# Block-sparse attention and a gated FFN in one kernel: keys dealt six to a partition, the first tile's mask added by TensorE, and a new table of scheduling priorities

## The chip, the cores and the metric

The kernel runs on one core of one Trainium2 chip. The metric is the device time of one execution in microseconds (us); the kernel before takes 277.04 us, the median of ten runs (276.79 to 277.46). Next to the times stands one profiled execution, from which all durations below are taken.

## The reference

Attention with a block mask, and behind it a feed-forward layer with a Swish gate:

```
B, H, S, D = 4, 8, 768, 64          # q, k, v: float32
scores = q @ k^T / sqrt(D)
mask   = blocks of 32: |i-j| <= 1, first and last block row and column,
         and three sampled key blocks for each query block
attn   = softmax(where(mask, scores, -1e9)) @ v        # [B, H, S, D]
x      = attn.transpose(0, 2, 1, 3).reshape(3072, 512)
h      = x @ w_in                                      # w_in  [512, 2048]
g      = h * sigmoid(beta * h)
out    = g @ w_out                                     # w_out [2048, 512]
```

The mask is the same for all batches and heads; only `sampled_blocks` (24x3 integers) makes it depend on an input.

## The kernel before

**Attention.** Two heads of a batch make a pair; there are sixteen pairs x, four to a batch. q, k and v of a pair are loaded as float32 into staging tiles `st_q`, `st_k`, `st_v`, cast to float16 on DVE or POOL (`s_q`, `s_k`, `va`), and q and k are turned so that the head's 64 features lie on partitions (`qX`, `kX`). The first four pairs are turned on PE and copied out of PSUM ("turn", "turn cp"); the others by a transposing DMA from SP's queue. A token (or key) index is written as (group g of 3, partition p of 128, c of 2): two neighbouring rows stand on a partition, so one piece of a load is 2 x 64 x 4 = 512 bytes.

A unit is one pair and one query tile, of n = 256 or 512 queries; batch 0 has a 256 tile and then a 512 tile, and each has four units. A unit's score step ("sc") makes one double bank of PSUM, 128 keys by 1024 scores for two heads; the two heads' matmuls use 64 rows of the array each. With n = 256 a unit has three steps of four 256-column matmuls, with n = 512 six steps of two 512-column matmuls. ACT takes the exponential of a step ("ex", tile `et`, 128x1024), DVE multiplies it with the 0/1 mask `mask01` ("mk"). When all steps of a unit are masked, PE multiplies with v ("av", 24 matmuls of 65 columns for each 256 queries; the 65th column holds the sums), DVE takes reciprocals and scales ("norm", tile `xst`), and the result is turned (on PE for batch 0 and the last pair, else by a transposing DMA) into `xT_sb`.

**The mask.** `sampled_blocks` is loaded first; a few small DVE operations make a 24x24 block mask, PE turns it, PE spreads it over key partitions with the `onehot` matrix (built on POOL at the start), and three copies on POOL ("spread") widen it to `mask01`, 128 x 3 x 384.

**The FFN.** `add_moe` handles a block of 256 or 512 tokens: sixteen groups of four matmuls with `w_in` ("hp"), a tanh on ACT for each ("th"), a multiply on DVE ("gm", tile `g`), then for each 128 tokens sixteen matmuls with `w_out` ("op"), a copy to `osb` on ACT or DVE, and a store from SP. The blocks are 256, five times 512, and 256 tokens. The weights are loaded and cast by four DMAs from POOL's queue of 2 MB of HBM data each. The first is held back by a one-element POOL copy that waits for the key load of pair 3 (`W_GATE`), and the loads of pair 4 are held back the same way until halves of `w_out` are there.

**The order.** All this is entered as nodes with engine, duration, dependencies and buffers, and `order_of` writes out one order for all engines by a list scheduling: of the nodes that can start it takes the one with the least start time plus a bias for its kind (`BIAS`). `MOST` limits how many PSUM banks a kind may hold, `SLOTS` gives the number of buffers of each tile. Each engine then runs its list in order; semaphores do the waiting. Nearly all operations are recorded through one helper and show as line 208 in the profile; the loads are lines 474 and 477, the weight loads 452 and 458, POOL's casts 497, the transposing DMAs 514 and 666, the stores 725.

Of the kernel before, what the change touches and what calls it, by code (L numbers as in the profile page):

```python
# [23 lines left out]
class Node:  # L24


    def __init__(self, kind, eng, dur, lat, emit, deps=(), take=(), use=(), moved=0,
                 rows=128, port=False, at=0.0, place=0.0):
        self.kind, self.place = kind, place
        self.eng = eng if isinstance(eng, tuple) else (eng,)  # L30
        self.dur = dur if isinstance(dur, dict) else {e: dur for e in self.eng}
        self.tail, self.emit = lat, emit
        self.deps = [d if isinstance(d, tuple) else (d, 0.0) for d in deps if d is not None]
        self.take, self.use, self.moved = list(take), list(take) + list(use), moved
        self.rows, self.port, self.at = rows, port, at
        for b in self.use:
            b.users += 1
        self.start = self.done = self.on = None


BIAS = {"av": -69, "beta": -455, "cast": 94, "dma": -1239, "ex": 257, "gm": -727, "hp": -468,
        "load": 1496, "lone sc": 331, "mask": -1415, "mk": 241, "next sc": 94, "norm": -152,
        "op": -13, "op on": -70, "osb": 284, "sc": -204, "spread": -316, "th": 422,
        "turn": -3422, "turn cp": -88, "two sc": -72, "weights": 774, "x cp": -31,
        "x turn": -102}

W_GATE = (3, "k")
# [12 lines left out]
MOST = {"av": 8, "hp": 6, "sc": 3}  # L60
# [31 lines left out]
def order_of(nodes, free, slots):  # L92
# [7 lines left out]
    left, after, at_dep = {}, {}, {}  # L100
    todo = []
# [8 lines left out]
    while todo:  # L110
        best = None
        for n in todo:
# [21 lines left out]
            for e in n.eng:  # L134
# [3 lines left out]
                bias = BIAS[n.kind]  # L138
                if n.rows == 64:
                    if rows == 64:  # L140
                        bias += BIAS["next sc"]
                    else:
                        room = sum(whole(bank, d, n_start) for d in range(len(bank) // 2))
                        bias += BIAS["lone sc"] if room < 2 else BIAS["two sc"] if room < 3 else 0
# [12 lines left out]
        if n.moved:  # L157
            other = "POOL" if e == "SP" else "SP"
            t, rest, rate = max(wire[e], start + DMA_FIRST[e]), n.moved, RATE[e]
            if e == "SP" and wire[other] > t:  # L160
                both = min(rest, (wire[other] - t) * SHARED)
                wire[other] += both / RATE[other]
                t, rest = t + both / SHARED, rest - both
            wire[e] = t + rest / rate
            n.done = wire[e] + DMA_LAST
        else:
# [74 lines left out]
def kernel(  # L241
# [29 lines left out]
    SLOTS = {"st_k": 2, "st_q": 5, "st_v": 5, "s16_k": 4, "s16_q": 2, "set": 4, "va": 4,  # L271
             "et": 13, "xst": 5, "recip": 7, "t_sb": 6, "g": 2, "osb": 3, "sc": 4}
# [36 lines left out]
    onehot = persist.tile([NB, NG, P], FP16, name="onehot")  # L309
    mask16 = persist.tile([NB, NB], FP16, name="mask16")  # L310
    mask_t = persist.tile([NB, NB], FP16, name="mask_t")
    mask_kb = persist.tile([P, NG, NB], FP16, name="mask_kb")
    mask01 = persist.tile([P, NG, NG * P], FP16, name="mask01")
# [23 lines left out]
    def emit_first():  # L337
# [6 lines left out]
        nc.vector.memset(warm, 0.0)  # L344

# [7 lines left out]
        nc.gpsimd.memset(onehot, 1.0)  # L353
        nc.gpsimd.affine_select(out=onehot, in_=onehot, pattern=[[CG * P, NG], [CG, P]],
                                compare_op=ALU.is_ge, fill=0.0, base=0,
                                channel_multiplier=-BLK)
        nc.gpsimd.affine_select(out=onehot, in_=onehot, pattern=[[-CG * P, NG], [-CG, P]],
                                compare_op=ALU.is_ge, fill=0.0, base=BLK - 1,
                                channel_multiplier=BLK)
# [15 lines left out]
    nodes = []  # L375

    def add(*a, **kw):
        n = Node(*a, **{"place": len(nodes) * 1e-3, **kw})
        nodes.append(n)
        return n  # L380

    mask_of = {}

    def add_mask():
# [3 lines left out]
        def mb(eng):  # L388
            dve.tensor_copy(out=sb_f32, in_=sb_i32)
            for r in range(3):  # L390
                dve.scalar_tensor_tensor(out=mask_blk if r < 2 else mask16, in0=iota_j,
                                               scalar=sb_f32[:, r:r + 1], in1=mask_blk,
                                               op0=ALU.is_equal, op1=ALU.max)

        def mt():
            pe.matmul(at(tb)[0:NB, 0:NB], lhsT=mask16, rhs=identity[0:NB, 0:NB],
                             start=True, stop=True)
# [4 lines left out]
        def km():  # L402
            for g in range(NG):
                pe.matmul(at(kb)[:, g * NB:(g + 1) * NB], lhsT=onehot[:, g], rhs=mask_t,
                                 start=True, stop=True)

        def kmc(eng):
            copy_on(eng)(out=mask_kb.rearrange("p c j -> p (c j)"), in_=at(kb)[:, 0:NG * NB])
# [8 lines left out]
        def spread(eng, g):  # L417
# [6 lines left out]
                    [P, NG, P // w, w]))  # L424
        n_mb = add("mask", "DVE", 950, 90, mb, at=4200.0)
        n_mt = add("mask", "PE", 60, 200, mt, deps=[n_mb], take=[tb], rows=32)
        n_mtc = add("mask", ("ACT", "DVE"), {"ACT": 200, "DVE": 100}, 100, mtc, deps=[n_mt], use=[tb])
        n_km = add("mask", "PE", 350, 200, km, deps=[n_mtc], take=[kb], rows=32)
        n_kmc = add("mask", ("ACT", "DVE"), {"ACT": 250, "DVE": 220}, 100, kmc, deps=[n_km], use=[kb])
        for g in range(NG):  # L430
            mask_of[g] = add("mask" if g == 0 else "spread", ("DVE", "POOL"),
                             {"DVE": 460, "POOL": 450}, 80,
# [11 lines left out]
    def add_weights(gate):  # L444
        st, load = gate

        def shut():
            nc.gpsimd.tensor_copy(out=w_in_sb[0:1, 0, 0:1], in_=at(st)[0:1, 0, 0:1])
        gate = add("weights", "POOL", 600, 50, shut, deps=[load], use=[st])
        for i in range(2):  # L450
            def wi(i=i):
                nc.gpsimd.dma_start(out=w_in_sb[:, :, i * 1024:(i + 1) * 1024],
                                    in_=w_in_r[:, :, i * 1024:(i + 1) * 1024])
            w_in_of[i] = add("weights", "POOL", 1000, 0, wi,
                            deps=[gate if i == 0 else (w_in_of[0], -1e9)], moved=2097152, port=True)
        for i in range(2):
            def wo(i=i):
                nc.gpsimd.dma_start(out=w_out_sb[:, i * 8:(i + 1) * 8, :],
                                    in_=w_out_r[:, i * 8:(i + 1) * 8, :])
            w_out_of[i] = add("weights", "POOL", 1200, 0, wo, deps=[(w_in_of[1], -1e9)],  # L460
                              moved=2097152, port=True)
# [4 lines left out]
    def add_load(nm, x, st, lo, hi, gate, more=False):  # L466
# [3 lines left out]
        def load():  # L470
            hg = src[b, 2 * j:2 * j + 2].rearrange("h (g p c) d -> p (h g) (c d)", g=NG, p=P)
# [6 lines left out]
        deps = [(d, -1e9) for d in last_load + begin]  # L478
        kw = {"use" if more else "take": [st]}
        if gate is not None:  # L480
            def shut():
                nc.gpsimd.tensor_copy(out=at(st)[0:1, 0, lo * D:lo * D + 1],
                                      in_=w_out_sb[0:1, gate * 8, 0:1])
            deps.append(add("weights", "POOL", 600, 50, shut, deps=[w_out_of[gate]], take=[st]))
            kw = {"use": [st]}
        last_load[:] = [add("load", "SP", 500 if hi - lo in (NC, CG) else 1000, 0, load, deps=deps,
                             moved=68000 * (hi - lo) + (170000 if x == 0 and nm == "v" else 0),
                             **kw)]
        return last_load[0]
# [13 lines left out]
    def add_half(x, nm, kq, lo, hi, first, gate, at_work=None):  # L503
# [4 lines left out]
        load = add_load(nm, x, st, lo, hi, gate, at_work and lo > 0)  # L508
        if x < NPAIR and lo == 0:
            loads[x, nm] = st, load  # L510
# [22 lines left out]
    def add_prep(x, gates=(None, None, None)):  # L533
# [18 lines left out]
        if x < NPAIR:  # L552
            loads[x, "v"] = st, lv
# [7 lines left out]
    def tile_steps(x, q0, n):  # L561
# [5 lines left out]
        for kc0 in range(0, NC, kn):  # L567
# [3 lines left out]
            def mm(sc=sc, kc0=kc0):  # L571
                kX, qX = at(kq)
                for i in range(kn):
                    for hh in range(2):
                        pe.matmul(
                            at(sc)[:, hh, i * n:(i + 1) * n],
# [3 lines left out]
                            start=True, stop=True)  # L580
# [6 lines left out]
            def mk(eng, et=et, kc0=kc0):  # L587
                w = n // CG
                e = at(et).rearrange("p h (r q) -> p (h r) q", q=w)
                m = mask01[:, kc0 // CG, q0 // CG:q0 // CG + w].unsqueeze(1).to_broadcast(  # L590
                    [P, 2 * CG * kn, w])
# [3 lines left out]
            steps.append((x, q0, k_of, sc, et, mm, ex, mk,  # L595
                          [mask_of[g] for g in range(q0 // (CG * P), (q0 + n) // (CG * P))]))
# [4 lines left out]
    def add_step(step, unit):  # L601
        x, q0, k_of, sc, et, mm, ex, mk, masks = step
        r = prep[x]
        g = add("sc", "PE", 218, 180, mm, deps=[(t, SLACK if x >= N_PE_TURN else 0)
# [4 lines left out]
        e = add("ex", "ACT", 927, 100, ex, deps=[g], take=[et], use=[sc])  # L609
        return add("mk", "DVE", 612, 80, mk, deps=[e] + masks, use=[et], port=True)  # L610

    def add_tail(x, q0, n, ets, masked):
# [6 lines left out]
        for half in range(nq // 2):  # L619
# [5 lines left out]
            def av(half=half, av_ap=av_ap):  # L625
                a = av_ap()
                for i in range(2):
                    qc = half * 2 + i
                    for hh in range(2):
                        for kc in range(NC):  # L630
                            at0 = (kc % kn) * n + (qc % CG) * (n // CG) + qc // CG * P
# [18 lines left out]
        if b == 0 or x == len(pairs) - 1:  # L650
# [22 lines left out]
    def add_moe(t0, n, gi):  # L673
# [3 lines left out]
        for f in range(N_FFC):  # L677
# [17 lines left out]
            h = add("hp", "PE", w, 180, hp, deps=set(xs + [w_in_of[f // 8]]), take=[hb],  # L695
# [4 lines left out]
        for ts in range(n // P):  # L700
            ob, sb = Buf("mm"), Buf("osb")
            prev = None
            for qq in range(4):
                def op(ts=ts, qq=qq, ob=ob):
                    for f in range(qq * 4, qq * 4 + 4):
                        pe.matmul(at(ob), lhsT=at(gb)[:, f, ts * P:(ts + 1) * P],
                                         rhs=w_out_sb[:, f, :],
                                         start=(f == 0), stop=(f == N_FFC - 1))
# [102 lines left out]
```

The softmax here doesn't subtract the row's maximum and nothing guards it: scores larger than these inputs give would overflow.

## Time and profile before

| | |
|---|---|
| median of ten runs | 277.04 us |
| profiled execution: time | 276.87 us |
| profiled execution: span of its instructions | 275.2 us |
| PE busy | 259.4 us (94%) |
| ACT busy | 217.2 us (79%) |
| DVE busy | 209.5 us (76%) |
| POOL busy | 31.8 us (12%) |
| DMA packets | 72882, of which 68756 under 2 KB |

1.67 us of the profiled execution lie outside its span. PE is TensorE's matmuls, PEld its weight loads, DVE is VectorE, ACT ScalarE, POOL GpSimd, SP the engine whose queue issues most DMAs. Busy matmuls include those that run at a lower rate, so PE's busy time isn't all needed work.

### The profile page before, as it was taken

To read this page: it belongs to the slowest core of one execution; us is meant where nothing else is said; L and a number is where in the kernel's file an instruction comes from. 1 tells how busy PE (TensorE), PEld (TensorE's weight loads), DVE (VectorE), ACT (ScalarE), POOL (GpSimd) and SP (SyncE) were. 2 spreads that over 40 slices of the span, in tenths; PEclk is the share of its full clock that TensorE was granted. 3 is DMA by queue.
4 is the path that set the end of the run, shared out by engine and by line. 5 is a ranking of instruction groups with operands and counts; after the bars stand their busy time and mean duration, and the time that the engine had idled before them with its cause. 6 is when DMAs were issued, how large, how long until landed. Compare 5 with 4: busy or idle time off the path is not lost.

```text
span 275.2 us, 6172 instructions
## 1 busy us (share of the span) xinstructions
PE 259.4 (94%) x2455; PEld 139.6 (51%) x2455; DVE 209.5 (76%) x416; ACT 217.2 (79%) x284; POOL 31.8 (12%) x53
## 2 busy tenths in 40 slices
PE   6678999969999999999999999999999999999993
PEld 2544674544455464455464444444545644567441
DVE  4888999998897798798988787978787877628000
ACT  4799998998789988789988788987798977529110
POOL 7143001043200111210010211030000000000000
PEclk9999999999999999999999999999999999999999
DMA  6999995599521798896576529481121200020222
GB/s 177 292 269 215 206 203 148 153 274 194 149 44 52 203 155 232 135 244 137 165 200 166 120 61 258 88 209 24 55 62 54 44 12 0 13 86 2 77 76 77
DMA packets 72882, 36.66 MB, mean 133 GB/s; under 512 B 29828, under 2 KB 68756, under 8 KB 72852
## 3 DMA queue, kind: packets, MB, share of 16 engines
q1 hardware_dynamic: 69600, 32.06, 48.5%
q0 software_dynamic: 3136, 4.19, 8.6%
q8 instruction: 19, 0.31, 0.5%
q14 instruction: 11, 0.09, 0.1%
q10 hardware_dynamic: 116, 0.01, 0.0%
HBM read 27.27 MB, written 6.29 MB: 122 GB/s over the span
## 4 chain that ended last, share of the span: by engine, by line
PE 78%; DVE 8%; DMA 6%; ACT 4%; SPq 2%; issue 1%; POOL 0%; DVEq 0%; ACTq 0%; POOLq 0%
PE sc L208 78%; DVE et L208 4%; DMA st_q<-in_q_dram 3%; ACT et L208 3%; DMA st_k<-in_k_dram 3%; DVE xst L208 1%; DMA sb_i<-in_sampled_blocks_dram 1%; SPq L474 1%; DVE recip L208 1%; ACT osb L208 0%; SPq L514 0%; DVE kX L208 0%; DVE xT_sb L208 0%; DVE s_q L208 0%; POOL s_k L497 0%
## 5 line engine op out<-in xcount | busy, mean ns | idle before, releaser
L208 ACT ACTIVATE et<-sc 128x1024 f16<-128x1024 f32 x144 | 136.4, 1043 | 14.2 <-PE sc L208 13.6
L208 DVE TENSOR_TENSOR et<-et,mask 128x1024 f16<-128x1024 f16 x144 | 95.0, 694 | 8.4 <-ACT et L208 8.3
L208 PE MATMUL sc<-w_out_sb,g 128*128 128x512 f16 x384 | 90.0, 379 | 0.0
L208 PE MATMUL sc<-xT_sb,w_in_sb 128*128 128x512 f16 (+1 forms) x448 | 84.3, 349 | 1.1 <-DVE xT_sb L208 1.0
L208 ACT ACTIVATE t_sb<-sc,beta_h_sb 128x512 f16<-128x512 f32 (+1 forms) x112 | 68.2, 649 | 17.1 <-PE sc L208 17.0
L208 DVE SCALAR_TENSOR_TENSOR g<-t_sb,sc 128x512 f16<-128x512 f16 (+1 forms) x112 | 67.7, 612 | 16.0 <-ACT t_sb L208 15.5
L208 PEld LDWEIGHTS <-w_in_sb 128*128 128x128 f16 x448 | 43.8, 98 | 40.7 <-issue 1.5
L208 PEld LDWEIGHTS <-g 128*128 128x128 f16 x384 | 34.6, 98 | 43.2 <-issue 7.5
L208 PE MATMUL sc<-qX,kX 64*128 64x256 f16 (+1 forms) x384 | 44.0, 339 | 4.9 <-ACT qX L208 2.1
L208 PEld LDWEIGHTS <-et 128*128 128x128 f16 x1152 | 39.7, 98 | 10.0 <-issue 6.8
L208 PE MATMUL sc<-va,et 128*128 128x65 f16 x1152 | 42.4, 194 | 1.4 <-ACT et L208 1.0
L208 PEld LDWEIGHTS <-kX 64*128 64x128 f16 x384 | 16.4, 98 | 26.7 <-issue 19.2
L208 ACT ACTIVATE osb<-sc 128x512 f32<-128x512 f32 x18 | 10.9, 608 | 17.9 <-PE sc L208 17.9
L208 DVE TENSOR_TENSOR xst<-sc,recip 128x256 f16<-128x256 f32 x48 | 20.4, 424 | 1.8 <-DVE recip L208 0.2
L208 DVE RECIPROCAL recip<-sc 128x4 f32<-128x4 f32 x48 | 8.7, 181 | 10.4 <-PE sc L208 8.8
L497 POOL CAST s_k<-st_k 128x768 f16<-128x768 f32 (+1 forms) x11 | 8.0, 729 | 74.1 <-DMA st_k<-in_k_dram 74.1
L497 POOL CAST s_q<-st_q 128x768 f16<-128x768 f32 (+2 forms) x11 | 8.8, 798 | 38.8 <-DMA st_q<-in_q_dram 36.6
L497 POOL CAST va<-st_v 128x768 f16<-128x768 f32 x7 | 6.1, 868 | 17.9 <-PE sc L208 13.9
L208 DVE CAST va<-st_v 128x768 f16<-128x768 f32 x9 | 5.2, 583 | 0.2 <-DMA st_v<-in_v_dram 0.2
L208 PE MATMUL sc<-identity,s_k 128*128 128x128 f16 x24 | 3.3, 283 | 1.9 <-ACT et L208 1.2
L208 DVE CAST s_q<-st_q 128x768 f16<-128x768 f32 (+2 forms) x9 | 4.1, 456 | 0.5 <-DMA st_q<-in_q_dram 0.5
L208 DVE COPY xT_sb<-sc 128x256 f16<-128x256 f16 (+1 forms) x9 | 3.1, 346 | 1.8 <-PE sc L208 1.8
(53 smaller groups left out, 44.5 us busy)
## 6 DMA issues: line engine op xcount, KB each, us to landing
st_v<-in_v_dram SPq DMA_DIRECT2D x16, 384.0 KB, 5.3
out_dram<-osb SPq DMA_DIRECT2D x24, 256.0 KB, 2.3
st_k<-in_k_dram SPq DMA_DIRECT2D x15, 384.0 KB, 4.4
st_q<-in_q_dram SPq DMA_DIRECT2D x12, 384.0 KB, 4.6
w_in_sb<-in_moe_w_in_dram POOLq DMA_DIRECT2D x2, 1024.0 KB, 10.3
w_out_sb<-in_moe_w_out_dram POOLq DMA_DIRECT2D x2, 1024.0 KB, 16.5
st_q<-in_q_dram SPq DMA_DIRECT2D x12, 128.0 KB, 5.3
st_k<-in_k_dram SPq DMA_DIRECT2D x3, 128.0 KB, 2.7
```

Of the source, the lines that this page charges most:

```text
L208: r = f(*a, **kw)
L474: nc.sync.dma_start(out=o, in_=hg)
L497: e(out=at(dst)[:, :, :, 0:D] if nm == "v" else by_chunk(dst, lo, hi), in_=src)
```

## The change

1. **Key layout.** Keys are dealt six to a partition (key = 6p + c), so k and v of a pair are loaded in pieces of 6 x 64 x 4 = 1536 bytes; q keeps 512 bytes, and the three part loads of pair 0's keys do too. With it the mask has one row per key chunk: `mask01` and `onehot` get six chunks instead of three groups, and columns of a score step are ordered query parity, key chunk, query.
2. **First tile's mask on PE.** The four units of the first tile (`N_PEMASK = 4`) get no DVE multiply. Ahead of each score matmul a matmul of the same size adds 0 or -30000 to PSUM (`onehot` times `shut_qk`), and the score matmul accumulates on it.
3. **Priorities.** `BIAS` has one value per batch and kind; `MOST` and `SLOTS` have new values; the early loads follow a list (`ORDER`); the scheduler's model of SP's queue gets eight lanes.
4. **Last store.** The last 128 tokens are computed, copied and stored in two halves of 256 columns.

The gate of the weights (the key load of pair 3) and their four pieces are as before; so are the gates of pair 4's loads.

```diff
-BIAS = {"av": -69, "beta": -455, "cast": 94, "dma": -1239, "ex": 257, "gm": -727, ...
+BIAS = {"av": (-633, -431, -677, -2885),
...
+ORDER = "k0a q0 k0b k0c v0 k1 q1 v1 k2 q2 v2 k3 q3 v3 r0 r1 r2 r3"
+N_PEMASK = 4
+SHUT = 30000.0
...
-MOST = {"av": 8, "hp": 6, "sc": 3}
+MOST = {"av": 29, "hp": 77, "sc": 2}
...
-    SLOTS = {"st_k": 2, "st_q": 5, "st_v": 5, "s16_k": 4, "s16_q": 2, "set": 4, "va": 4,
-             "et": 13, "xst": 5, "recip": 7, "t_sb": 6, "g": 2, "osb": 3, "sc": 4}
+    SLOTS = {"st_k": 2, "st_q": 3, "st_v": 2, "s16_k": 6, "s16_q": 3, "set": 5, "va": 5,
+             "et": 10, "xst": 2, "recip": 54, "t_sb": 14, "g": 2, "osb": 6, "sc": 4}
...
-        nc.gpsimd.memset(onehot, 1.0)
-        nc.gpsimd.affine_select(out=onehot, ...          # twice, 24x384
+        for h in range(2):
+            nc.gpsimd.tensor_copy(out=onehot_t[r]...     # 64x768 each
+        nc.gpsimd.tensor_copy(out=onehot.rearrange("b c p -> b p c"), ...   # 128x768
...
+        def neg(eng):
+            o = shut_qk.rearrange("b g (m r) -> b (g m) r", r=BLK // CG)
+            i = at(tb)[:, 0:NB].unsqueeze(2).to_broadcast([P, NB, BLK // CG])
+            ...                                          # 30000 * (mask - 1), 128x384, ACT or DVE
...
+            if nm != "q":
+                hk = src[b, 2 * j:2 * j + 2].rearrange("h (p c) d -> p h (c d)", p=P)
+                nc.sync.dma_start(out=at(st)[:, :, lo * D:hi * D], in_=hk[:, :, lo * D:hi * D])
+                return
...
                 for i in range(kn):
                     for hh in range(2):
+                        if by_pe:
+                            r = slice(hh * D, (hh + 1) * D)
+                            pe.matmul(s_of(hh, i), lhsT=onehot[r, kc0 + i, :],
+                                rhs=shut_qk[r, q0 // (CG * P):(q0 + n) // (CG * P)].unsqueeze(
+                                    1).to_broadcast([D, CG, n // (CG * P), P]),
+                                start=True, stop=False)
+                    for hh in range(2):
                         pe.matmul(
-                            at(sc)[:, hh, i * n:(i + 1) * n],
+                            s_of(hh, i),
...
-                            start=True, stop=True)
+                            start=not by_pe, stop=True)
...
+            end = t0 + ts * P + P == N_TOK
+            w = D_MODEL // 2 if end else D_MODEL
+            for m0 in range(0, D_MODEL, w):              # op, copy and store of w columns
```

## The prediction

> **What bounds the kernel now.** I read the busy shares of the page first, then a table by stage that I cut where the chain of waits turns from mixed to PE alone, then the timeline of the first 61 us. The page:
>
> ```profile
> PE   6678999969999999999999999999999999999993
> DVE  4888999998897798798988787978787877628000
> ACT  4799998998789988789988788987798977529110
> PEclk9999999999999999999999999999999999999999
> ```
>
> PE has holes at three places only: the first four slices, one slice at 55 us, and the end. The stages (length, then busy time of PE, PEld, DVE, ACT, POOL with instruction counts, granted clock, DMA share, GB/s):
>
> ```profile
> 15.90:30.04 14.14, 10.27 (x140) 6.26 (x139) 12.54 (x30) 13.90 (x18) 4.45 (x6) 1.00 1.15 228
> 30.04:53.20 23.16, 23.08 (x276) 15.05 (x277) 22.03 (x49) 21.45 (x35) 1.32 (x3) 1.00 0.81 171
> 53.20:60.99 7.79, 5.13 (x81) 3.38 (x81) 7.28 (x16) 7.67 (x10) 2.75 (x3) 1.00 0.99 260
> 60.99:126.00 65.01, 64.91 (x598) 32.86 (x598) 54.66 (x99) 56.00 (x72) 9.25 (x11) 1.00 0.78 158
> 126.00:270.90 144.90, 144.72 (x1272) 75.23 (x1271) 102.52 (x193) 107.70 (x141) 6.71 (x8) 1.00 0.35 90
> ```
>
> The same table has PE busy 2.58, 3.75 and 5.01 us in 0 to 5, 5 to 10 and 10 to 15.90. So PE is idle 8.4 us before 30.04, where the first FFN block begins, 2.7 us in 53.20 to 60.99, some 0.4 us elsewhere, and 4.30 us after its last matmul. From 61 us on only less PE work can shorten the span; before 30 us ACT (13.90 of 14.14) and DVE (12.54) are the full engines. Four rows of the timeline (start, length, engine, line, operation, count, idle time before):
>
> ```profile
> 14.57 1.46 PE L208 MATMUL sc<-qX,kX 64*128 64x256 f16 x12
> 16.17 0.67 DVE L208 TENSOR_TENSOR et<-et,mask 128x1024 f16<-128x1024 f16 x1
> 17.82 0.83 PE L208 MATMUL sc<-qX,kX 64*128 64x256 f16 x12 [1.11 <-ACT qX L208]
> 30.04 7.39 PE L208 MATMUL sc<-xT_sb,w_in_sb 128*128 128x256 f16 x64 [0.45 <-DVE xT_sb L208]
> ```
>
> The same twelve score matmuls take 1.46 us until 15.9 us and 0.83 us after, although the clock row says full: PE begins at half its rate. Summing that excess over the rows before 15.9 (three score units 1.9, first "av" 0.6, turns 1.7) gives 4.2 us. Hence the sum of before: needed PE work 259.4 - 4.2 = 255.2; idle plus excess before the first FFN 8.4 + 4.2 = 12.6; second hole 2.7; rest 0.4; last matmul at 270.9; tail 4.3; span 275.2. Another 1.67 us lie outside the span (276.87), and the median is 0.17 us above that execution.
>
> **First tile's mask on PE.** Twelve DVE products go: 12 x 0.68 = 8.2 us of DVE before 30 us, where the chain of waits passes through them and through the casts and copies queued with them. PE gets 12 x 4 = 48 matmuls of the same shape as the score ones: 48 x 0.83/12 = 3.3 us at full rate, 5.8 us at 1.46/12. ACT's chain is what is late next: first exponential at 6.93 + 0.49 (four half-rate matmuls ahead of it) = 7.4; twelve at 0.95 make 18.8; three qX copies at 0.37 on ACT make 19.9; then the last unit's "av" 0.93, reciprocal 0.18, scaling 0.42, two turns 0.28, xT copy 0.29 and six hops of 0.05 give 22.3 for the first FFN matmul if nothing waits. The other bound is 30.04, nothing won: half-rate score steps now take 0.98 us each, just over an exponential. Between 22.3 and 30.04 I take the middle, 26.2, because ACT had 2.9 us idle between 5 and 20 us that this does not remove, and because the first half of `w_in`, issued at 15.06 and landing in 9.9 to 10.6 us, is there only at 25.7. So 3.8 us earlier. What stood in those 3.8 us, about 3.8/0.95 = 4 score steps of tile 1 at 0.28, slips behind: 1.1 us. Idle plus excess before the first FFN becomes 26.2 - (17.4 + 3.3 - 1.1) = 6.6 us, 17.4 being the 21.6 busy less 4.2.
>
> The page "TensorE: Matmul & The Clock Gate" (Part 1) of the Trainium skill says that the array runs at half rate until about 3.4 us of sustained activity, judged in free-running windows. In this trace PE was busy without a break from 12.0 to 15.9 before the rate changed, which agrees; by the rule the extra matmuls would end the half rate sooner, an estimated 2 us less excess and a sum near 272.
>
> **New wait.** The first tile's scores now wait for `shut_qk`, and "turns" of the next pair stand behind them on PE. The mask's turn ends at 4.90; the new copy of 128x384 from PSUM lies between ACT's 0.37 (128x256) and 0.64 (128x512), say 0.5, so it is done at 5.45, while qX is only copied at 5.63 and the first score matmul began at 6.28: no cost. Uncovered it would be up to 0.5 us at the very start.
>
> **POOL.** Three operations on `onehot` (0.41 + 0.51 + 0.56 = 1.5 us) become three copies of 768 columns; the nearest row is POOL's 128x768 cast, 0.85, so 2.55: POOL is free at 4.5, not 3.47. Its cast of `s_k` at 3.41 can go to DVE (0.35 us for 128x256), which is idle until 3.59: nothing; if the order leaves it on POOL, everything starts 1.1 us later. Widening `mask01` costs 3 x (0.85 - 0.51) = 1.0 us more, hidden since tile 1 is now its first reader and POOL was idle 2.9 us before 10.04; uncovered, one cast of `va` is later by that.
>
> **Loads of k and v.** Their packets become three times as long.
>
> ```profile
> 12.00:14.00 2.00, 2.00 (x28) 1.72 (x25) 1.59 (x4) 1.62 (x3) 0.00 (x0) 1.00 1.18 290
> 255.00:258.00 3.00, 3.00 (x16) 1.35 (x15) 0.00 (x0) 0.60 (x1) 0.00 (x0) 1.00 0.24 87
> 14.57 0.18 POOL L448 CAST w_in_sb<-st_k 1x1 f16<-1x1 f32 x1 [3.71 <-DMA st_k<-in_k_dram]
> ```
>
> At 512 bytes the engines are full (share 1.18) at 290 GB/s, 246 per unit of share; the stores with 2048-byte rows reach 87/0.24 = 363 per unit. They are writes, so this is only a bound: six whole loads (2.36 MB) lie before the gate at 14.57, 8.1 us at 290 GB/s, 5.5 us if faster by 363/246. The weights start 0 to 2.6 us sooner. In the likeliest case I book nothing: 26.2 is behind the first half's landing. It matters for the second half (20.71 + 10.6 = 31.3): matmuls of group 8 would be due at 26.2 + 32 x 0.112 = 29.8, and a late half leaves 1.5 us to be filled with tile 1's work.
>
> The page "DMA: Bandwidth & Descriptors" (Specifications) of the Trainium skill puts the smallest transfer at line rate at 512 bytes, which speaks against this part: by it the longer rows bring nothing, and the sum is as I make it. The bound from the stores would allow about 1 us more, and no run here shows loads of 1536 bytes.
>
> **Order and buffers.** The new priorities move every step; after 61 us PE has 209.6 of 209.9 us filled, so there is nothing to win and something to lose. `xst` with two buffers is covered: a transposing DMA lands in 2.4 us (5.8 at worst), units come every 209.9/24 = 8.7 us. So is `st_v` with two: a load lands in 5.3 us. The hole at 55 us stays in the likeliest case: ACT is busy 7.67 of 7.79 there, and the DVE time won is spent earlier.
>
> **Last store.** The last copy is 128x256, 0.37 (nearest ACT row) instead of 0.60; the store of half the bytes lands 0 to 0.3 us sooner (2.0 to 2.3 in the rows); 32 matmuls at 0.112 instead of 16 at 0.218 cost 0.1. Tail 4.3 to 4.0, work +0.1.
>
> **Sum.** Work 255.2 + 3.3 + 0.1 = 258.6; 6.6 before the first FFN; hole 2.7; rest 0.4: last matmul at 268.3. Tail 4.0: span 272.3. With 1.67 and 0.17: 274.1 us.
>
> **Rivals.** A (0.50), as summed. Its own range is from a first FFN at 22.5 (7.5 earlier, 2.2 slipping: 271.5) to one at 29 (275.9).
>
> D (0.20): the freed DVE takes ACT's copies (4 us before 61), the weights come sooner, and the second hole closes as well: 274.1 - 2.7 = 271.4, less about 1 for earlier weights, 270.4. For it: ACT did 45 exponentials before 61 us, only 36 of which the second FFN block needs. Against: ACT is as full as DVE.
>
> B (0.12): the change does not do what it says. PE, at half rate with doubled score steps, takes DVE's place, and the first FFN stays near 30: only the tail is won, 276.7; at worst, with 0.49 more on each of twelve steps uncovered and half of it filled elsewhere, 279. For it: PE is busy 5.01 of 5.90 in 10 to 15.9.
>
> C (0.18), slower: `et` falls from 13 to 10 buffers. A 512 unit holds six until its "av" ends, so ACT can be four steps ahead instead of seven, 3.8 us, while an FFN block of 512 tokens keeps PE for 14 us and tile boundaries need the next unit at once. Its place is the four tile boundaries after 61 us, its price 2.7 us each (the hole at 55 us is the row), and it decides from two holes on: 274.1 + 5.4 = 279.5. Against it: ACT is idle 9 us in 61 to 126 and 37 after.
>
> **How the numbers follow.** This kernel's measurement can tell about 0.2%, 0.55 us. Faster: A 0.48, D 0.20, B 0.02, together 0.70. Same: A 0.02, B 0.06, 0.08. Slower: B 0.04, C 0.18, 0.22. The range 269.0 to 278.8 leaves out the far parts of D (0.07) and of C (0.11).
>
> **What would show it.** Right: the first FFN matmul before 28 us, DVE under 10 us busy in 15.9 to 30, PE's busy time up by 2 to 4 us, the gate of the weights before 14.57, no PE idle over 1 us after 61. Wrong: a first FFN at 30 or later, score units of 2.9 us beyond 16 us (half rate lasting), or idle time of PE before "av" in the later tiles, released by ACT's `et`. If PE's idle time before 61 falls under 6 us, D was the case.

## The result: slower by 0.4%, and the profile after

The changed kernel takes 278.04 us (median of 15 runs, 277.52 to 279.26) against 277.01 us for the kernel before in the same session: a ratio of 1.0042 [1.0030, 1.0054]. The forecast was 274.1 us and faster. The profiled execution took 278.68 us with a span of 276.8 us, so 1.88 us lie outside it. The busy tenths of the changed kernel, in forty slices:

```profile
PE   2699899998999999999999999999999999999994
DVE  8556889899988898889868987965666758863630
ACT  1479998989789888999988967757676678672741
POOL 8447001142020100201000013311000000000000
PEclk9999999999999999999999999999999999999999
```

The hole at 55 us is closed, but in the first slice (6.9 us) PE is now at 2 tenths and ACT at 1, where PE had 6 and ACT 4; DVE and POOL are at 8. The table by stage of the changed kernel, cut at its own first FFN matmul (29.40) and its last matmul (273.20); columns as in the prediction (length, busy time of PE, PEld, DVE, ACT, POOL, granted clock, DMA share, GB/s):

```profile
0.00:5.00 5.00, 1.89 (x4) 0.43 (x4) 3.81 (x13) 1.28 (x1) 4.13 (x12) 1.00 0.46 126
5.00:10.00 5.00, 0.65 (x10) 0.54 (x11) 3.58 (x6) 0.59 (x2) 3.46 (x6) 1.00 0.87 254
10.00:15.90 5.90, 5.24 (x49) 3.63 (x49) 3.60 (x9) 3.54 (x7) 1.88 (x3) 1.00 0.66 207
15.90:29.40 13.50, 12.45 (x214) 8.76 (x209) 8.33 (x23) 13.07 (x16) 8.07 (x12) 1.00 1.03 222
29.40:53.20 23.80, 23.00 (x270) 14.41 (x269) 21.16 (x46) 22.11 (x34) 2.80 (x6) 1.00 0.92 176
53.20:60.99 7.79, 7.47 (x90) 3.92 (x87) 7.03 (x15) 6.46 (x8) 2.13 (x3) 1.00 1.04 326
60.99:126.00 65.01, 63.88 (x622) 32.25 (x621) 58.07 (x109) 58.65 (x75) 8.81 (x10) 1.00 0.72 164
126.00:273.20 147.20, 147.19 (x1282) 77.04 (x1278) 101.92 (x193) 105.83 (x140) 7.60 (x10) 1.00 0.33 89
```

In 5 to 10 us PE works 0.65 us where it worked 3.75. Behind 15.9 the change does what it should: DVE has 8.33 us of work in 13.5 instead of 12.54 in 14.1. The timeline of the changed kernel says what stands in the first 12 us (start, length, engine, line, operation, count, idle time before and who ended it):

```profile
2.69 0.76 DVE L409 SCALAR_TENSOR_TENSOR mask_blk<-iota_i,mask_blk 24x24 f32<-24x24 f32 x1
3.48 0.17 DVE L407 SCALAR_TENSOR_TENSOR mask_blk<-iota_j,mask_blk 24x24 f32<-24x24 f32 x1
3.48 3.64 POOL L397 COPY onehot<-onehot_t 128x768 f16<-128x768 f16 x1
3.69 2.84 DVE L409 SCALAR_TENSOR_TENSOR mask_blk<-iota_i,mask_blk 24x24 f32<-24x24 f32 x1
6.46 0.98 DVE L244 CAST sb_f<-sb_i 24x3 f32<-24x3 int32 x1
8.57 0.20 PE L244 MATMUL sc<-identity,mask 24*128 24x24 f16 x1 [5.49 <-DVE mask L244]
8.80 0.49 ACT L244 ACTIVATE shut_qk<-sc 128x384 f16<-128x384 f32 x1 [4.94 <-PE sc L244]
12.05 1.94 ACT L244 ACTIVATE et<-sc 128x1024 f16<-128x1024 f32 x2 [0.81 <-PE sc L244]
16.70 0.18 POOL L519 CAST w_in_sb<-st_k 1x1 f16<-1x1 f32 x1 [0.21 <-DMA st_k<-in_k_dram]
19.30 1.67 POOL L508 DMA_DIRECT2D w_in_sb<-in_moe_w_in_dram  x2
29.26 0.46 PEld L244 LDWEIGHTS <-w_in_sb 128*128 128x128 f16 x4 [0.91 <-DMA w_in_sb<-in_moe_w_in_dram]
```

POOL's third `onehot` copy takes 3.64 us, not 0.85. Beside it an operation of DVE on 24x24 elements takes 2.84 us; one of the same kind and shape takes 0.17 at 3.48. The block mask is late by that, and by a cast behind it that takes 0.98 us (0.15 in the first experiment); PE waits 5.49 us for it, `shut_qk` is ready at 9.3 instead of the forecast 5.45, and the first exponential starts at 12.05 us (6.93 before). The key buffers come free later too: the weights' gate opens at 16.70 (14.57 before), their first DMA is issued at 19.30 (15.06), and the first FFN matmul finds them just landed.

### The profile page after: what moved, and what is told of

It reads as the page before. It is cut to its first block, busy times and chain, and to the rows that moved or that the text cites. A ratio compares the mean times of both kernels' runs of the same rounds, so it can differ in the third digit from the quotient of the medians.

```text
span 276.8 us, 6255 instructions
## 1 busy us (share of the span) xinstructions
PE 261.8 (95%) x2522; PEld 141.0 (51%) x2522; DVE 207.5 (75%) x409; ACT 211.9 (77%) x278; POOL 38.9 (14%) x58
## 2 busy tenths in 40 slices
DMA packets 57153, 36.65 MB, mean 132 GB/s; under 512 B 29844, under 2 KB 53156, under 8 KB 57124
## 4 chain that ended last, share of the span: by engine, by line
PE 89%; DVE 6%; ACT 2%; issue 1%; DVEq 0%; ACTq 0%
PE sc L244 89%; DVE et L244 2%; DVE mask_blk L409 1%; ACT et L244 1%; ACT t_sb L244 1%; DVE s_k L244 0%; DVE g L244 0%; DVE mask_blk L407 0%; DVE sb_f L244 0%; DVE xst L244 0%; DVE mask_blk L244 0%; ACT shut_qk L244 0%; DVE s_q L244 0%; DVE recip L244 0%; ACT osb L244 0%
## 5 line engine op out<-in xcount | busy, mean ns | idle before, releaser
L244 DVE TENSOR_TENSOR et<-et,mask 128x1024 f16<-128x1024 f16 x132 | 88.6, 710 | 4.4 <-ACT et L244 3.9
L244 PE MATMUL sc<-w_out_sb,g 128*128 128x512 f16 (+1 forms) x400 | 90.5, 371 | 0.6 <-DVE g L244 0.6
L244 PE MATMUL sc<-xT_sb,w_in_sb 128*128 128x512 f16 (+1 forms) x448 | 86.8, 349 | 1.8 <-ACT et L244 0.8
L244 DVE SCALAR_TENSOR_TENSOR g<-t_sb,sc 128x512 f16<-128x512 f16 (+1 forms) x112 | 65.0, 608 | 15.7 <-ACT t_sb L244 15.2
L244 PE MATMUL sc<-qX,kX 64*128 64x256 f16 (+1 forms) x384 | 46.4, 330 | 1.3 <-DVE s_k L244 0.7
L244 DVE TENSOR_TENSOR xst<-sc,recip 128x256 f16<-128x256 f32 x48 | 20.2, 423 | 1.4
L244 ACT ACTIVATE osb<-sc 128x512 f32<-128x512 f32 (+1 forms) x15 | 8.5, 568 | 15.5 <-PE sc L244 15.5
L244 DVE RECIPROCAL recip<-sc 128x4 f32<-128x4 f32 x48 | 8.7, 181 | 15.6 <-PE sc L244 14.1
L571 POOL CAST va<-st_v 128x768 f16<-128x768 f32 x11 | 9.6, 876 | 47.0 <-DMA st_v<-in_v_dram 30.1
L244 DVE TENSOR_SCALAR osb<-sc 128x512 f32<-128x512 f32 x10 | 6.9, 689 | 10.3 <-PE sc L244 10.1
L244 PE MATMUL sc<-shut_qk,onehot 64*128 64x256 f16 x48 | 7.1, 311 | 0.0
L244 DVE COPY kX<-sc 128x768 f16<-128x768 f16 (+1 forms) x5 | 2.3, 451 | 4.9 <-PE sc L244 4.9
```

The costliest lines, as they stand in the source:

```text
L244: r = f(*a, **kw)
L571: e(out=at(dst)[:, :, :, 0:D] if nm == "v" else by_chunk(dst, lo, hi), in_=src)
```

## The experiments

**Theory.** The price of the third copy and its hold on DVE make the start late, and the late start costs all that was won. **Rivals.** The late start is covered anyway and the loss comes from the mask matmuls on PE, from the new priorities and buffers behind 29 us, or from the half-rate PE at the start. Ratios are against the kernel before, run beside each. The experiments were measured in three groups, so times of different groups are compared by these ratios too.

**The copy on ACT, unchanged in form.**

```diff
-        nc.gpsimd.tensor_copy(out=onehot.rearrange("b c p -> b p c"),
-                              in_=onehot_t.rearrange("b (p c) -> b p c", c=NC))
+        nc.scalar.copy(out=onehot.rearrange("b c p -> b p c"),
+                       in_=onehot_t.rearrange("b (p c) -> b p c", c=NC))
```

> One line of the changed kernel differs: the 128x768 copy that deals onehot to six key chunks runs on ACT, idle then, not on POOL. Theory (POOL's 3.64 us copy holds back DVE's small mask operations, and the whole kernel starts 5 us late): the mask is ready before 6 us instead of 8.52, the first exponential starts at 7.5 to 8.5 instead of 12.05, and the time falls by 3 to 5 us to 273 to 275. Rival 1 (the extra PE work of the mask matmuls is what costs, the late start is cover for loads that are late anyway): first exponential earlier, but the time stays within 1 us of 278.0. Rival 2 (the new order loses in the later tiles): also within 1 us, with PE idle time moved behind 30 us.

Measured: 276.79 us, 0.9999 [0.9975, 1.0023]. Its timeline:

```profile
3.68 0.40 DVE L409 SCALAR_TENSOR_TENSOR mask_blk<-iota_i,mask_blk 24x24 f32<-24x24 f32 x1
3.66 0.39 POOL L571 CAST s_k<-st_k 128x256 f16<-128x256 f32 x1
3.88 3.61 ACT L397 COPY onehot<-onehot_t 128x768 f16<-128x768 f16 x1
5.21 0.19 PE L244 MATMUL sc<-identity,mask 24*128 24x24 f16 x1 [2.13 <-DVE mask L244]
6.99 0.81 ACT L244 ACTIVATE shut_qk<-sc 128x384 f16<-128x384 f32 x1
10.56 1.94 ACT L244 ACTIVATE et<-sc 128x1024 f16<-128x1024 f32 x2 [0.81 <-PE sc L244]
```

The copy is as long on ACT (3.61), but DVE's operation falls from 2.84 to 0.40 us and the mask reaches PE at 5.21 instead of 8.57. So it was POOL's copy that held DVE, not a slow operation of DVE; what is left of the hold, 0.40 for 0.17, ends with POOL's next operation, the cast of `s_k` (4.08 and 4.05). Now `shut_qk` stands behind the copy on ACT, and the first exponential gains only 1.5 us; the time stays 1.8 us above the range that was expected.

**The copy on POOL, with the stride on the read side.**

```diff
-        nc.gpsimd.tensor_copy(out=onehot.rearrange("b c p -> b p c"),
-                              in_=onehot_t.rearrange("b (p c) -> b p c", c=NC))
+        nc.gpsimd.tensor_copy(out=onehot, in_=onehot_t.rearrange("b (p c) -> b c p", c=NC))
```

> The same copy stays on POOL, but writes in order and reads with the stride, instead of the reverse; its bytes are the same. If the strided write makes it 3.64 us long, it now takes 0.85 to 1.3 us, DVE is released by 4.8 us, and the time falls to 274 to 276. If POOL's copy is long for another reason (held by DVE, or slow for any stride), it stays over 3 us and the time stays at 278.

Measured: 276.62 us, 0.9996 [0.9967, 1.0024]. Its timeline:

```profile
3.47 1.23 POOL L397 COPY onehot<-onehot_t 128x768 f16<-128x768 f16 x1
3.68 1.06 DVE L408 SCALAR_TENSOR_TENSOR mask_blk<-iota_i,mask_blk 24x24 f32<-24x24 f32 x1
4.86 1.69 DVE L244 SCALAR_TENSOR_TENSOR mask_blk<-iota_j,sb_f,mask_blk 24x24 f32<-24x24 f32 x2
6.90 0.20 PE L244 MATMUL sc<-identity,mask 24*128 24x24 f16 x1 [3.82 <-DVE mask L244]
```

The same bytes cost a third when each write goes to the next address and the read steps by 12 bytes, instead of writes that step by 256. DVE's operation still ends with POOL's copy (4.74 and 4.70), and DVE's next two take 1.69 us beside POOL's casts of `s_k` and `s_q` (4.83 to 6.25), where they took 0.53 in the first experiment. So the mask is at PE at 6.90, not at 5.21, and the first exponential at 10.38.

**Only the cost: the three copies put into the kernel before,** into spare tiles that nothing reads.

> The kernel before, with the changed kernel's three POOL copies (two of 64x768, one of 128x768 with strided writes) into spare tiles added behind its own onehot, nothing reading them. Theory: POOL's first cast of k and DVE's mask chain are held back by some 5 us, the first exponential starts at 10 to 12, and the time rises by 3 to 5 us to 280 to 282. Rivals 1 and 2: the start has slack, less than 1 us more.

Measured: 280.80 us, 1.0130 [1.0096, 1.0165]; the timeline:

```profile
4.14 3.87 DVE L208 SCALAR_TENSOR_TENSOR mask_blk<-iota_j,sb_f,mask_blk 24x24 f32<-24x24 f32 x2
5.01 3.60 POOL L367 COPY spare<-spare_t 128x768 f16<-128x768 f16 x1
8.96 0.40 PE L208 MATMUL sc<-identity,s_k 128*128 128x128 f16 x2 [5.80 <-POOL s_k L506]
11.32 1.02 ACT L208 ACTIVATE et<-sc 128x1024 f16<-128x1024 f32 x1 [0.33 <-PE sc L208]
```

Nothing but the copies is added, and 3.9 us are lost (276.92 beside it); first exponential (11.32) and first FFN matmul (34.26) are 4.2 to 4.4 us late. So the copies alone are enough for a loss of this size. But DVE is not the way here: in this order PE turns the keys first, and what it waits for, 5.80 us, is POOL's own late cast of `s_k` (at 8.33; the copies come on top of the old `onehot` operations).

**Both mends: the copy on ACT, stride on the read side.**

```diff
-        nc.gpsimd.tensor_copy(out=onehot.rearrange("b c p -> b p c"),
-                              in_=onehot_t.rearrange("b (p c) -> b p c", c=NC))
+        nc.scalar.copy(out=onehot, in_=onehot_t.rearrange("b (p c) -> b c p", c=NC))
```

> The changed kernel with the onehot copy on ACT and with the stride on the read side: POOL and DVE are both free of it, and it should take 0.8 to 1.3 us on ACT behind its table load. Theory (each us of start costs about one us of time): mask turned by 5.3, first exponential at 8.5 to 9.5 instead of 12.05 (10.6 and 10.4 in the first two runs), time 274.5 to 276. Rival 2 (the new order and the PE mask lose what the start wins): time stays at 276.6, where the first two runs are.

Measured: 275.64 us, 0.9929 [0.9901, 0.9958], faster than both kernels. Its timeline:

```profile
3.86 1.21 ACT L397 COPY onehot<-onehot_t 128x768 f16<-128x768 f16 x1
5.35 0.20 PE L244 MATMUL sc<-identity,mask 24*128 24x24 f16 x1 [2.27 <-DVE mask L244]
5.58 0.49 ACT L244 ACTIVATE shut_qk<-sc 128x384 f16<-128x384 f32 x1 [0.51 <-PE sc L244]
8.83 1.94 ACT L244 ACTIVATE et<-sc 128x1024 f16<-128x1024 f32 x2 [0.81 <-PE sc L244]
14.00 0.18 POOL L518 CAST w_in_sb<-st_k 1x1 f16<-1x1 f32 x1 [0.24 <-DMA st_k<-in_k_dram]
27.61 0.60 PE L244 MATMUL sc<-xT_sb,w_in_sb 128*128 128x256 f16 x4 [0.76 <-ACT et L244]
```

From the change as made to this kernel only one instruction differs; first exponential 12.05, 10.56 (copy on ACT), 8.83 go with 278.04, 276.79, 275.64 us, and with ratios of 1.0042, 0.9999, 0.9929.

**No mask on PE: the copy on ACT, `N_PEMASK = 0`,** the order planned anew.

> The first run's kernel with N_PEMASK = 0: the first tile's mask by DVE again, the order written anew for it. Theory: PE has 3.3 us less to do but DVE 8.2 us more before 30 us; as PE idles less than 7 us before the first FFN block there, the mask on PE is worth 0 to 2 us: 274 to 277. Rival 1 (mask matmuls are what costs): 2 us or more below the first run.

Measured: 282.93 us, 1.0211 [1.0179, 1.0244], first FFN matmul at 34.0 instead of 27.9 us. Beside the first experiment, the mask on PE is worth 6.1 us in this order (0 to 2 were expected), at the place where the forecast had it. Part of it may come by way of the clock: PE is busy 0.29 us in 28 to 30 us, and the granted clock is 0.51 in 30 to 32 and 0.63 in 32 to 34, an estimated 1.7 us (2 x 0.49 + 2 x 0.37) ahead of its first FFN matmul. The priorities stayed those chosen with it, so this is its worth in this table of priorities only.

**The old priorities on the second experiment** (old `BIAS` for all batches, old `MOST`, new buffers).

> The kernel of the second run with the old BIAS for all four batches and the old MOST; buffers, layout and PE mask as in the change. Theory (the order is worth something, but not what decides): 276 to 281. Rival 2 (the new order loses time in the later tiles): faster than the second run's 276.6 by over 1 us.

Measured: 298.47 us, 1.0754 [1.0702, 1.0807]; PE waits 12.9 us for ACT's `et`, and the granted clock is 0.966 on the mean. The new buffers need the new priorities; it tells nothing about what each is worth.

**Loads in 512-byte pieces,** by another access pattern on the second experiment.

> The kernel of the second run (POOL's copy with the stride on the read side), with each load of k and v described in pieces of 512 bytes again, all else the same. If long rows matter: packets rise to some 72000, the gate of the weights at 14.5 comes 1 to 2.5 us later, and the time rises by 0.5 to 2 us over the second run's 276.6. If 512 bytes is enough: packets rise, times of loads stay, and the time is within 0.5 us of it.

Measured: 276.85 us, 0.9982 [0.9955, 1.0010], with 57153 DMA packets, exactly as with long rows: the pieces were merged again, so it repeats the second experiment to 0.23 us and leaves its question open.

**Turns ahead of the mask, by a constraint on the planner,** on the kernel with both mends.

```diff
...
+    n_mt = mt_of[0]
+    for c in (prep[0]["k of"][0], prep[0]["q"]):
+        n_mt.deps.append((c.deps[0][0], -1e9))
```

> As the run before, and PE's list has the first turns of k and q ahead of the mask's turn, so that they don't stand behind a wait for the mask. Theory: first exponential at 7 to 8.5, first FFN matmul at 25 to 26.5, time 272.5 to 275, below the kernel before by 0.7 to 1.6%. Rival 2: no gain over the run before. As every early step may be planned in another order by this, 1 us either way is not read as anything.

`n_mt` is the mask's turn. Measured: 295.04 us, 1.0617 [1.0569, 1.0665]. The first exponential is at 8.3 us, but PE waits 11.1 us for `et` in 22 places (mean granted clock 0.982): one constraint at 5 us changed the order everywhere. An experiment on the start has to edit the finished order.

**The start improved further,** all three on the best kernel so far: twelve warming matmuls instead of four (`emit_warm(12)`); pair 0's first turns and copies moved ahead of the mask's turn in the finished order; both.

> The kernel with the onehot copy on ACT and the stride on the read side (275.64), with 12 instead of 4 matmuls on a zero tile at the start, where PE is idle from 3.1 to 5.35 us. Theory (what is left of the loss is PE at half rate with doubled score steps until 16 us): score units take 1.7 us instead of 2.8 from 11 us on at the latest, the first FFN matmul comes at 25 to 26.5 instead of 27.6, and the time falls by 1 to 3 us to 272.6 to 274.6. Rival (the half rate is cover for ACT and the loads): rate up sooner, time within 0.6 us of 275.6; if the mask's turn is held back by the added matmuls, up to 0.8 us more.

> The same base, with only pair 0's first turns of k and q and their two copies moved ahead of the mask's turn in the finished order, nothing else planned anew (the run that let the planner do it came out at 295). Theory (a us of start is worth about a us): first exponential at 7.6 to 8.0 instead of 8.83, time 274.3 to 275.3. Rival: within 0.3 us of 275.6, since the half rate or the loads take over.

> Both of these together. Theory: 271.8 to 274.2. Rival: no lower than the better of the two by more than 0.3 us.

Measured: 275.24 us, 0.9927 [0.9901, 0.9953]; 275.59 us, 0.9951 [0.9930, 0.9972]; 275.63 us, 0.9948 [0.9924, 0.9973]. None is told apart from 275.64. The timeline of the first (more warming):

```profile
7.54 0.28 PE L244 MATMUL sc<-shut_qk,onehot 64*128 64x256 f16 x2
8.22 1.94 ACT L244 ACTIVATE et<-sc 128x1024 f16<-128x1024 f32 x2 [0.32 <-PE sc L244]
26.07 0.61 PE L244 MATMUL sc<-xT_sb,w_in_sb 128*128 128x256 f16 x4 [1.18 <-DMA w_in_sb<-in_moe_w_in_dram]
```

Two score or mask matmuls take 0.28 us from the first on (0.40 to 0.42 in the changed kernel): there is no half rate left in the scores, and yet at most 0.4 us is won. PE now waits 1.18 us for the weights' DMA. With both edits the first FFN matmul comes at 25.23, a microsecond before the forecast 26.2; the waits of PE and the stage table of that kernel:

```profile
PE sc L244 <- DVE g L244: 2.4, 4, 1.5
```

```profile
61.00:126.00 65.00, 62.86 (x622) 31.99 (x620) 57.59 (x110) 57.32 (x74) 6.64 (x8) 1.00 0.68 159
```

The columns of the first are total, times and longest. PE waits 2.4 us for DVE's `g` (1.3 in the changed kernel), and is idle 2.1 us in 61 to 126 (1.1 there, 1.0 in the kernel with both mends): of the 2.4 us by which the first FFN comes earlier than with both mends alone, 1.1 are given back in this stage.

**No mask matmuls at all,** on the kernel with both edits: the 48 matmuls are left out, so the first tile goes unmasked; the order stays.

> As the run before with the 48 mask matmuls left out and nothing in their place, so the first tile is not masked; the order is the same. It prices PE's share of the change in a fixed order. Theory (3.3 us of PE work, of which about half hides in idle time before the first FFN block): 1 to 2.5 us less. If the mask matmuls were free there: within 0.5 us. If they are the decisive cost: 3.3 us or more.

Measured: 276.13 us, 0.9962 [0.9937, 0.9987] beside 0.9948 [0.9924, 0.9973] with them. The stage from 10 to 16 us, first without the mask matmuls, then with them:

```profile
10.00:16.00 6.00, 4.75 (x52) 3.69 (x54) 3.20 (x7) 4.33 (x7) 2.47 (x5) 0.51 0.89 280
10.00:16.00 6.00, 5.12 (x96) 4.17 (x95) 3.47 (x9) 4.90 (x8) 2.83 (x5) 1.00 0.97 318
```

Without them the granted clock (third from the end) is 0.51 there, not 1.00, and the first FFN matmul comes later, at 26.62. So the run doesn't price the matmuls: what they cost and what the lower clock costs stand against each other. But leaving them out brings nothing back in this order, and the kernel with both mends has no loss with all of them in; as the cause of the loss this rival falls.

## Why the prediction was wrong, step by step

**The step that failed: POOL.** The third `onehot` copy was priced at 0.85 us from the nearest row, a cast that writes straight on; it writes with a stride of 256 bytes and took 3.64. Its price was then judged only by who waits in POOL's own queue ("nothing, or 1.1 us"), and no one asked what it does to DVE beside it. The profile of before had the answer in two rows:

```profile
2.18 0.51 POOL L354 TENSOR_SCALAR_AFFINE_SELECT onehot<-onehot 24x384 f16<-24x384 f16 x1
2.19 0.53 DVE L368 SCALAR_TENSOR_TENSOR mask_blk<-iota_j,mask_blk 24x24 f32<-24x24 f32 x1
```

The same operation of DVE took 0.17 us at 1.71. "New wait: no cost" fell with the price, since that took the mask's time from the profile of before. The first exponential came at 12.05, where 7.4 was forecast. Changing only this copy (its engine and its strides) moves the ratio from 1.0042 to 0.9929, which shows the cause of the loss. Two ways lead from the copy to the start. In the changed kernel PE waited for the mask and turned the keys behind it, at 9.79; POOL's late casts by themselves (`s_k` at 6.85 instead of 3.41, `s_q` done at 7.77) would have let it turn them from 7.8 on. In the kernel before with the copies the casts were the way.

The rows bear out a rule that the forecast passed over. The page "SBUF — State Buffer" of the Trainium skill (Who interferes with whom) says that DVE and GpSimd share a pair of ports as an exclusive lock, and that a DVE instruction with two SBUF inputs contends with a GpSimd instruction that reads SBUF; the held operation has two such inputs. The same page (Door 1) notes 16-byte lines in SBUF, with a penalty for each access that crosses to a new one. With 256-byte steps every write goes to a new line, with 12-byte steps three reads of four do, and the copies take 3.6 and 1.2 us (0.83 for POOL's copy of that size into `mask01`, whose writes are straight). The direction agrees; the rule alone doesn't give the factor of three, and no run here varies the step further.

**The sum, term by term.** The forecast had the first FFN matmul at 26.2, 239.0 us of PE work behind it (258.6 less the 19.6 ahead), 3.1 of idle time there and a tail of 4.0: 272.3. The changed kernel has 29.40, 241.5 (23.00 + 7.47 + 63.88 + 147.19), 0.80 + 0.32 + 1.13 = 2.3 and 3.6: 276.8, the span. So the late first FFN is 3.2 of the miss and the work behind it 2.5, less 0.8 and 0.4 that went better (this execution is 0.6 us above the median). The kernel with both mends has 27.61, 241.6, 1.9 and 3.6: with the copy mended 1.4 of the 3.2 stay (twelve warming matmuls bring 26.07), and the 2.5 are not the copy's doing. So without the failed step the sum would still have been 0.9 to 1.5 us low: 274.1 for 275.64, or for 275.0 by its ratio.

**The work behind the first FFN, mis-sized.** It was to rise by 1.2 us, 1.1 of tile 1's work that slips and 0.1 at the end; it rose by 3.7, from 237.8 (23.08 + 5.13 + 64.91 + 144.72). The slip itself was nearly right: counted in the traces, 12 score matmuls of 512 columns stand ahead of the first FFN instead of 22, so five steps slipped, not four, and four turns of q; by the forecast's 0.28 a step and 0.4 for the turns, that is at most 1.9 us with the end. The rest is the same matmuls in another order. Before, the first 64 with `w_in` run in one piece (7.39 us at 30.04); after, score steps stand between them:

```profile
29.40 0.60 PE L244 MATMUL sc<-xT_sb,w_in_sb 128*128 128x256 f16 x4 [0.76 <-ACT et L244]
29.93 0.39 PE L244 MATMUL sc<-qX,kX 64*128 64x512 f16 x2
30.25 1.05 PE L244 MATMUL sc<-xT_sb,w_in_sb 128*128 128x256 f16 x8
```

From start to start four take 0.53 us, where 4 x 0.112 = 0.45 was their price, and a score step 0.32, where two more score matmuls in a row add 0.22 (0.61 for four, 0.39 for two). Behind the first FFN the order goes 26 times from one of these kinds to the other, 3 times before; 23 more at some 0.1 us are an estimated 2.3 us, enough for the 1.8 that are left. The forecast said of the new priorities "something to lose" and booked nothing. No run varies this alone.

**The half rate.** The run with both edits has the same matmuls ahead of its first FFN, all at full rate: 20.36 us busy less 4.08 for twelve warming matmuls plus 1.89 for four are 18.2 of needed work, where 19.6 was forecast. (Its rows of two score or mask matmuls start 0.11 us apart, so 48 mask matmuls take 2.6 us, not 3.3.) So the excess, the time lost at half rate, was 20.2 - 18.2 = 2.0 in the changed kernel and 21.7 - 18.2 = 3.5 in the mended one, and idle time plus excess in the changed kernel 9.2 + 2.0 = 11.2, forecast 6.6. In the trace of before PE is busy without a break from 10.89, not 12.0, to the change of rate at 15.9. By the page "TensorE: Matmul & The Clock Gate" (Part 1) of the Trainium skill the added matmuls were estimated to save 2 us of the 4.2 us of excess. Excess fell by 2.2 in the changed kernel and by 0.7 in the mended one, and no time near 272 came of it.

**Small slips in the sums.** A's upper end comes to 276.1 by its own terms, not 275.9, and B's worst to 279.6, not 279; C's 14 us for an FFN block are its `w_in` matmuls alone. Nothing hangs on these.

**Right.** PE's busy time rose by 2.4 (2 to 4 was said), DVE fell under 10 us in 15.9 to 30, the mask's move gained at the start (the run without it starts its FFN 6.1 us later), and the tail won 0.7. **The hole at 55 us** closed, against the forecast, as rival D had it (why was not traced); 1.0 of those 2.3 us came back as idle time in 61 to 126. **Rival B** has the right look, a first FFN near 30, by the wrong cause: full-rate scores changed the time by at most 0.4 us. **Rival C**, which held most of the chance of slower, fell: PE waits for `et` 1.1 us in all, 3.6 before. The chance of slower, 0.22, held no case that begins at POOL.

**Loads.** Forecast: nothing booked, the gate 0 to 2.6 us earlier. It opened at 16.70, for the key buffers were freed late, and at 14.00 in the mended kernel. The rows of long loads, first of the changed kernel, then of the second experiment (last two columns: DMA share, GB/s):

```profile
14.00:16.00 2.00, 1.34 (x17) 0.96 (x16) 1.23 (x3) 0.78 (x2) 0.38 (x1) 1.00 1.02 372
```

```profile
12.00:14.00 2.00, 1.15 (x20) 0.95 (x19) 1.56 (x3) 1.23 (x3) 0.77 (x1) 1.00 1.05 359
```

That is 342 to 365 GB/s for a full share, where 512-byte rows gave 246. The rule cited from "DMA: Bandwidth & Descriptors" (Specifications) of the Trainium skill, full rate from 512 bytes on, is not what these windows show; they mix other transfers in, and the run that was to isolate the size did not.

## What to carry to other kernels

Price a copy by a row with the same strides, and when a step moves onto POOL or grows there, look at what DVE does in that window: the queue that it delays may not be its own. When an early chain sets the start, test it by editing that one instruction in the finished order, since a planner that runs anew changes everything. And once the start is mended, ask what is late next: here the weights' DMA and the wait for `g` took over after 2.4 us (278.04 to 275.64). Price an order also by how often PE goes from one kind of matmul to another.

## What the runs showed of the hardware that was not expected

- A 128x768 f16 copy with writes 256 bytes apart takes 3.64 us on POOL and 3.61 on ACT; with reads 12 bytes apart and straight writes 1.23 and 1.21.
- A 24x24 operation of DVE with two SBUF inputs takes 0.17 us at its shortest, 0.40 and 0.53 beside operations of POOL of 0.39 and 0.51, 1.06 beside POOL's copy of 1.23 and 2.84 beside that of 3.64.
- Twelve warming matmuls instead of four bring the scores to full rate from the first on; the granted clock reads full in both cases.
- With the 48 mask matmuls left out, the granted clock in 10 to 16 us is 0.51 instead of 1.00, though PE is busy 4.75 of the 6 us.
- A step of two 512-column score matmuls of 64 rows takes 0.32 us up to the next start when it stands between matmuls with `w_in`; in a row of its own kind a step adds 0.22.
